# Batch 0's k and q loaded by longer pieces, turned in eighteen turns each, k ahead of p, and short products of zeros ahead of and between the turns

## The chip, the core and the metric

The kernel runs on one core of a Trainium2 chip. The metric is device time in microseconds (us), the median of several executions. The engines are named as in the profile: PE is TensorE's matmul, PEld its weight load, DVE is VectorE, ACT ScalarE, POOL GpSimd, SP the queue from which all DMAs are issued.

## The reference

Eight batches, eight heads, 576 tokens of 64 numbers. For each head a packed attention and an attention over its result, then a gated network over all tokens (x is 4608 x 512):

```
p_packed = sm_attn(p, k, v)              # p has 32 rows a head
out = sm_attn(q, p_packed, p_packed)
a = x @ w_a ;  b = x @ w_b               # 512 x 1536 each
return (a * b @ w_out)                   # 1536 x 512
```

All tensors are float32. The kernel keeps the exactness with products of high and low parts.

## The kernel before

Batches are worked on one after the other, the attention of the next batch beside the network of this one. The first stage of a batch (`stage1`) multiplies p by k, takes a softmax over 576 tokens and multiplies by v; the second (`stage2`) multiplies q by the packed result, takes a softmax over 32 and leaves its parts a_hi and a_lo. The network uses that the packed result has only 32 rows a head: `g_tiles` multiplies it by the weights (ghi, glo, two feature tiles at a time), and `mm1` multiplies ghi, glo by a_hi, a_lo. `mm2_part` is the product with w_out.

The weights come as 36 raw pieces of 512 KB, and each is turned into numbers by three steps, named by letters in the tables: A (`high_word`, on ACT), B (`low_word`, on ACT, DVE or POOL by the digit 0, 1 or 2 of `WAYS`) and C (`both_words`, on DVE). A `g_tiles` of two feature tiles needs the C of four pieces. The raw pieces have twelve buffers.

The order of every engine's queue is written out by hand. `FIRST` is the order of the loads on SP, `START` that of the work before the network begins, `PLAN_0` and `PLAN` that of the work between the half tiles of `mm1`. In `START`, k0 to k4 and q0 to q4 are the turns of k and q (`turn_first`: a PE turn of 128 columns against the identity `ident`, and copies on DVE or ACT by the digit of `TURN`), T0 and P0 the turns of p and of the packed result, S0 and S1 the first products of `stage1` for even and odd heads, r0 and r1 its later steps, s0 and s1 the steps of `stage2`, g the first `g_tiles`, and W nine products of 128x512 columns whose result nobody reads.

In PSUM x and m are pairs of buffers and s a single one of two banks. Batch 0 and 1 have their tokens in an order that `store_first` undoes when the results are written.

Of the kernel before, what the change touches and what calls it, by code (L numbers as in the profile page):

```python
# [8 lines left out]
F32 = mybir.dt.float32  # L9
# [10 lines left out]
def tile_packed_attn_gated_ffn(  # L20
# [72 lines left out]
    def bank():  # L93
        return ps_x.tile([P, 512], F32, name="x")
# [31 lines left out]

    firsts = {}

    def load_first(src, key, part):

        if part < 2:
            t = scratch.tile([P, R, 4 * D], F32, name=f"{key}n{part}")
            nc.sync.dma_start(
                out=t, in_=src[0, R * part:R * part + R, 0:4 * P, :].rearrange("h (p i) d -> p h (i d)", i=4))
        else:
            t = scratch.tile([P, H, 2 * D], F32, name=f"{key}n{part}")
            nc.sync.dma_start(out=t[0:TR], in_=src[0, :, 4 * P:S, :].rearrange("h (p u) d -> p h (u d)", u=2))
        firsts[key, part] = t  # L140

    def turn_first(key, n):

        if (0, key) not in xTs:
            pool = scratch if key == "q" else ld
            xTs[0, key] = [pool.tile([P, R, HS], F32, name=f"xT{i}") for i in range(2)]
        copy = (nc.vector.tensor_copy, nc.scalar.copy)[int(TURN["kq".index(key) * 5 + n])]
        x = bank_pair()[:, 0, :] if n in (2, 3) else bank()
        if n < 4:
            h = 2 * (n % 2)  # L150
            for i in range(4):
                nc.tensor.transpose(  # L152
                    x[:, P * i:P * i + P], firsts[key, n // 2][:, h + i // 2, P * (i % 2):P * (i % 2) + P], ident)
            copy(out=xTs[0, key][n // 2][:, h:h + 2, 0:2 * P], in_=x.rearrange("p (h t) -> p h t", h=2))
            return
        for h in range(H):
            nc.tensor.transpose(x[:, TR * h:TR * h + TR], firsts[key, 2][0:TR, h, :], ident[0:TR, 0:TR])
        for i in range(2):
            copy(out=xTs[0, key][i][:, :, 2 * P:HS], in_=x[:, P * i:P * i + P].rearrange("p (h t) -> p h t", h=R))
# [105 lines left out]
    def stage1(b, e):  # L265
# [185 lines left out]
    def store_first(ob, x, i):  # L451

        for u in range(2):
            if x < 8:
                rows = out[0:4 * P].rearrange("(a l i) n -> a i l n", a=4, i=4)[x % 4, 2 * (x // 4) + u]
            else:
                rows = out[4 * P:S].rearrange("(l u) n -> u l n", u=2)[u]
            nc.sync.dma_start(out=rows, in_=ob[i + TL * u:i + TL * u + TL])
# [68 lines left out]
    PLAN_0 = ("A | C C | B A B A | B C C B C | A A | C | B | C B A T0 k0 Lp2 A | A A B B C Lq0 | C C k1 | A B A | "  # L527
# [447 lines left out]
```

## Time and profile before

| | |
|---|---|
| median of 3 executions | 711.39 us (710.65 to 711.81) |
| the profiled execution: its own time, its span | 711.86 us, 710.1 us |
| PE busy | 696.6 us, 98% of the span |
| DVE, ACT, POOL busy | 451.5, 361.6, 418.2 us |
| first product of `mm1` | 35.14 us from the span's start |

The span runs from the first to the last instruction, and the time is some 1.8 us longer. A busy PE is one that has an instruction under way, which is not yet a PE at its peak. In the timelines a bracket at a row's end says how long the engine stood idle before the row, and what ended the wait. The chain that ended last lies on PE for 92% of the span and on DVE for 5%.

### The profile page before, as it was taken

The numbers are of one execution on the slowest core, as the hardware profiler recorded it, in microseconds if no ns is written. First come the engines' busy times: TensorE is split into PE (matmuls) and PEld (weight loads), VectorE is DVE, ScalarE is ACT, GpSimd is POOL, SyncE is SP. The second block draws the span as 40 slices with busy tenths as digits, with TensorE's granted clock in tenths as the row PEclk, the third lists the DMA queues.
The fourth block names the chain that finished last, engine by engine and source line by source line (L and its number), as shares of the span: only waits on it lengthen the run. The fifth ranks groups of instructions, "written<-read, shape, count | busy, mean of one in ns | idle before, by whom it ended". The sixth has DMA issues, their size and how long they took to land.

```text
span 710.1 us, 14172 instructions
## 1 busy us (share of the span) xinstructions
PE 696.6 (98%) x5546; PEld 573.4 (81%) x5546; DVE 451.5 (64%) x823; ACT 361.6 (51%) x729; POOL 418.2 (59%) x322
## 2 busy tenths in 40 slices
PE   5899999999999999999999999999999999999998
PEld 4488877888878878888888788788888888888886
DVE  3788755367456679665875678765785667754342
ACT  2788754454344455645554456555555446544420
POOL 0496753337334787745874589566775578856520
PEclk9999999999999999999999999999999999999999
DMA  8999967852344735546443563456245323133002
GB/s 250 386 270 308 259 114 247 247 112 90 93 114 141 207 86 158 135 125 152 141 102 123 148 184 93 122 171 159 75 110 169 105 90 119 60 111 127 1 1 74
DMA packets 181507, 102.63 MB, mean 145 GB/s; under 512 B 145728, under 2 KB 163904, under 8 KB 176064
## 3 DMA queue, kind: packets, MB, share of 16 engines
q1 hardware_dynamic: 181440, 101.73, 50.8%
q8 instruction: 43, 0.70, 0.4%
q14 instruction: 24, 0.20, 0.1%
HBM read 85.98 MB, written 15.73 MB: 143 GB/s over the span
## 4 chain that ended last, share of the span: by engine, by line
PE 92%; DVE 5%; issue 1%; ACT 1%; DMA 1%; SPq 0%; DVEq 0%; ACTq 0%
PE x L742 36%; PE m L784 27%; PE m L407 11%; PE m L433 5%; PE x L798 4%; PE s L319 2%; PE s L334 1%; PE x L389 1%; PE s L273 1%; DVE a_lo L91 1%; PE s L309 1%; DMA kn<-in_k_dram 1%; DVE part L752 1%; PE x L152 0%; PE m L152 0%
## 5 line engine op out<-in xcount | busy, mean ns | idle before, releaser
L742 PE MATMUL x<-wo,h_hi 128*128 128x512 f32 (+1 forms) x776 | 249.4, 391 | 0.0
L91 POOL TENSOR_TENSOR h_lo<-asb,h_hi 128x576 fp32r<-128x576 f32 x96 | 140.4, 1464 | 80.7 <-ACT h_hi L829 43.3
L742 PEld LDWEIGHTS x<-wo,h_hi 128*128 128x128 f32 x776 | 140.9, 188 | 22.0 <-ACT part L750 0.8
L742 PE MATMUL x<-wo,h_lo 128*128 128x512 f32 (+1 forms) x388 | 152.1, 392 | 0.0
L91 POOL TENSOR_TENSOR G_lo<-gs,G_hi 128x640 fp32r<-128x640 f32 x72 | 112.7, 1572 | 30.1 <-ACT G_hi L819 29.8
L742 PEld LDWEIGHTS x<-wo,h_lo 128*128 128x128 f32 x388 | 72.9, 188 | 11.7
L91 POOL TENSOR_TENSOR A_lo<-gs,A_hi 128x256 fp32r<-128x256 f32 x36 | 27.6, 766 | 89.6 <-ACT A_hi L807 89.6
L866 DVE TENSOR_TENSOR d<-m,d 128x576 f32<-128x576 f32 (+1 forms) x73 | 54.1, 741 | 34.7 <-ACT d L862 33.9
L879 DVE TENSOR_TENSOR asb<-m,d 128x288 f32<-128x288 f32 x72 | 32.5, 451 | 64.1 <-ACT c L875 60.7
L875 ACT COPY c<-m 128x288 f32<-128x288 f32 x72 | 28.8, 400 | 83.5 <-PE m L784 83.5
L752 DVE TENSOR_TENSOR part<-x,part 128x512 f32<-128x512 f32 (+1 forms) x65 | 44.1, 678 | 38.4 <-PE x L742 38.4
L784 PE MATMUL m<-tx_hi,G_hi 128*128 128x288 f32 x216 | 63.8, 295 | 0.0
L784 PE MATMUL m<-tx_hi,G_lo 128*128 128x288 f32 x216 | 63.6, 295 | 0.0
L784 PE MATMUL m<-tx_lo,G_hi 128*128 128x288 f32 x216 | 63.2, 293 | 0.0
L804 ACT COPY gs<-x 128x512 f32<-128x512 f32 x35 | 20.6, 588 | 81.9 <-PE x L798 80.6
L819 ACT CAST G_hi<-gs 128x640 fp32r<-128x640 f32 x72 | 52.2, 729 | 15.1 <-POOL gs L813 14.5
L862 ACT COPY d<-m 128x576 f32<-128x576 f32 (+1 forms) x73 | 46.7, 639 | 19.4 <-PE m L784 18.9
L829 ACT CAST h_hi<-asb 128x576 fp32r<-128x576 f32 x72 | 49.0, 680 | 11.5 <-DVE asb L893 11.5
L784 PEld LDWEIGHTS m<-a_hi,G_hi 128*128 128x128 f32 x144 | 27.0, 187 | 31.9 <-issue 17.4
L813 POOL TENSOR_TENSOR gs<-gs 128x512 f32<-128x512 f32 x36 | 46.6, 1293 | 2.9 <-DVE gs L810 2.8
L784 PE MATMUL m<-a_hi,G_hi 128*128 128x288 f32 x144 | 46.6, 324 | 0.0
L407 PE MATMUL m<-a_hi,ghi 128*128 128x288 f32 x192 | 43.2, 306 | 1.5 <-ACT ghi L395 1.5
(176 smaller groups left out, 1545.4 us busy)
## 6 DMA issues: line engine op xcount, KB each, us to landing
wr<-w_kept SPq DMA_DIRECT2D x36, 1024.0 KB, 5.0
nat<-in_k_dram SPq DMA_DIRECT2D x56, 144.0 KB, 4.7
nat<-in_q_dram SPq DMA_DIRECT2D x56, 144.0 KB, 5.3
vt<-in_v_dram SPq DMA_DIRECT2D x28, 256.0 KB, 3.9
out_dram<-part SPq DMA_DIRECT2D x27, 256.0 KB, 2.0
raw<-in_moe_w_a_dram SPq DMA_DIRECT2D x12, 512.0 KB, 7.7
raw<-in_moe_w_b_dram SPq DMA_DIRECT2D x12, 512.0 KB, 7.0
raw<-in_moe_w_out_dram SPq DMA_DIRECT2D x12, 512.0 KB, 7.2
```

The costliest lines, as they stand in the source:

```text
L91: return eng.tensor_tensor(out=dst, in0=src, in1=hi.bitcast(F32), op=ALU.subtract)
L407: nc.tensor.matmul(out=ps[:, half, 0:HS], lhsT=gt[:, kt, ft % 4, cols], rhs=at[:, kt, HS * half:HS * half + HS], start=(n == 0 and kt == 0 ...
L433: nc.tensor.matmul(out=o[:, cols], lhsT=ht[:, c0:c0 + P], rhs=wt[:, cols], start=(ft == 0 and n == 0), stop=(ft == NFT - 1 and n == 2))
L742: nc.tensor.matmul(out=o[:, cols], lhsT=ht[:, c0:c0 + P], rhs=wt[:, cols], start=(ft == fts[0] and n == 0), stop=end)
L752: nc.vector.tensor_tensor(out=parts[i][:, cols], in0=o[:, cols], in1=parts[i][:, cols], op=ALU.add)
L784: nc.tensor.matmul(out=bank[:, n % 2, 0:HS], lhsT=g, rhs=t, start=(first and i == 0), stop=(i == 2), skip_group_check=True)
L813: nc.gpsimd.tensor_tensor(out=gs[:, 2:4].rearrange("p a u f -> p a (u f)"), in0=gs[:, 0:2].rearrange("p a u f -> p a (u f)"), in1=s2.unsqu ...
L819: nc.scalar.copy(out=G_hi[:, n % 3], in_=gs[:, 1:6, n % 2])
L829: nc.scalar.copy(out=view(h_hi[ft]), in_=src)
L862: nc.scalar.copy(out=d[:, both], in_=X[:, both, 0:HS])
L866: nc.vector.tensor_tensor(out=d[:, both], in0=V[:, both, 0:HS], in1=d[:, both], op=ALU.add)
L879: nc.vector.tensor_tensor(out=hf[:, 1], in0=X[:, k0, 0:HS], in1=d[:, k0], op=ALU.mult)
```

## The change

The loads of k and q of batch 0 are two DMAs each in place of three: a partition holds a head and 36 neighbouring tokens, 16 of them (4 KB) by the first DMA and 20 (5 KB) by the second. All eighteen turns are now full 128x128 turns; before there were sixteen and eight of 32 rows. The copies write four or one neighbouring columns at a time in the order that the products want. k is loaded ahead of p. In `stage1` the last 32 columns of batch 0 are read with a step. W is gone; `wake` multiplies a tile of zeros by itself, 128x128, so many times as the number behind X, Y or Z says (into an x, s or m buffer): 24 times ahead of the first turn, nine in the first softmax, and 45 in the second stage. The tables START, PLAN_0, WAYS and TURN are new; B is on DVE for 15 pieces (7 before), on POOL for 5 (10) and on ACT for 16 (19). The stores of the first batch's results go in other pieces.

```diff
+    zero = scratch.tile([P, P], F32, name="zero")
+    nc.vector.memset(zero, 0.0)
...
     def load_first(src, key, part):
-        if part < 2:
-            t = scratch.tile([P, R, 4 * D], F32, name=f"{key}n{part}")
...
+        lo, n = ((0, 16), (16, 20))[part]
+        t = scratch.tile([P, n * D], F32, name=f"{key}n{part}")
+        rows = src[0].rearrange("h (g i) d -> (h g) (i d)", i=36)
+        nc.sync.dma_start(out=t, in_=rows[:, lo * D:(lo + n) * D])
...
     def turn_first(key, n):
+        pairs = [range(n, 8, 2), range(n, 8, 2), range(10, 18, 2), range(11, 18, 2), range(8, 10)][n]
+        for i, pair in enumerate(pairs):
+            c = P * (pair % 8 if pair < 8 else pair - 8)
+            nc.tensor.transpose(x[:, P * i:P * i + P], firsts[key, int(pair > 7)][:, c:c + P], ident)
         if n < 4:
+            m = pairs[0] // 2
+            out = wide[key][:, :, n % 2, :, m:m + 4]
+            copy(out=out, in_=x.rearrange("p (m h g) -> p h g m", m=4, h=H))
...
-    def warm(n=9):
+    def wake(kind, n):
-        x = bank_pair()[:, 0, :]
-        t = firsts["k", 0].rearrange("p h t -> p (h t)")
+        x = (bank() if kind == "X" else bank_pair(kind == "Y")[:, 0])[:, 0:P]
         for _ in range(n):
-            nc.tensor.matmul(out=x, lhsT=ident, rhs=t[:, 0:512], start=True, stop=True)
+            nc.tensor.matmul(out=x, lhsT=zero, rhs=zero, start=True, stop=True)
...
-    FIRST = ("p0 k0 k2 k1 q0 v0 q1 v1 q2 w1 w1 w1 w1 w1 w1 w1 w1 w1 w1 w1")
-    START = ("T0 k0 k4 k1 k3 k2 q0 S0 S1 r0 r1 q1 r1 r0 r0 r1 r0 q2 r1 q3 q4 P0 s0 B s1 W A s0 B A A s0 s0 B s1 C "
+    FIRST = ("k0 k1 p0 q0 q1 v0 v1 w1 w1 w1 w1 w1 w1 w1 w1 w1 w1 w1")
+    START = ("Y4 X6 X14 k0 k1 k2 T0 k3 k4 q1 S0 S1 r0 X4 r1 Z3 q0 r1 r0 Y2 r0 r1 q2 r0 r1 q3 q4 P0 s0 B s0 B X3 "
```

The queue of PE from the program's first instruction to the first softmax. Here p_nat, kn and qn are the loaded tiles, a row of the form `x<-ident,kn` is a turn, and `s<-xT,pT` or `s<-kT,pT` are S0's products. Before:

```order
L250 MATMUL x<-ident,p_nat 128x128 x2
L152 MATMUL x<-ident,kn_108 128x128 x4
L157 MATMUL x<-ident,kn_110 128x32 x8
L152 MATMUL x<-ident,kn_108 128x128 x4
L152 MATMUL m<-ident,kn_112 128x128 x8
L152 MATMUL x<-ident,qn_114 128x128 x4
L273 MATMUL s<-xT_154,pT 32x288 x2
```

And in the change:

```order
L591 MATMUL s<-zero 128x128 x4
L591 MATMUL x<-zero 128x128 x20
L152 MATMUL x<-ident,kn_107 128x128 x8
L152 MATMUL m<-ident,kn_109 128x128 x4
L250 MATMUL x<-ident,p_nat 128x128 x2
L152 MATMUL m<-ident,kn_109 128x128 x4
L152 MATMUL x<-ident,kn_109 128x128 x2
L152 MATMUL x<-ident,qn_114 128x128 x4
L280 MATMUL s<-kT,pT 32x256 x4
```

Twenty-four products of zeros stand at the head of the queue, p's turn has moved behind twelve of k's, and k takes 18 turns in place of 24.

The queue of PE from S1's last product to the turn of the first softmax (`a_0`). Before:

```order
L273 MATMUL m<-xT_155,pT 32x32 x2
L152 MATMUL x<-ident,qn_114 128x128 x4
L309 MATMUL x<-ident,a_0_228 128x128 x4
L310 MATMUL x<-ident,a_0_228 64x128
L309 MATMUL m<-ident,a_1_234 128x128 x4
L310 MATMUL m<-ident,a_1_234 64x128
L319 MATMUL x<-vt,a1T_247 32x64 x20
L152 MATMUL m<-ident,qn_120 128x128 x4
```

And in the change:

```order
L280 MATMUL m<-kT,pT 32x32 x4
L591 MATMUL x<-zero 128x128 x4
L591 MATMUL m<-zero 128x128 x3
L152 MATMUL x<-ident,qn_114 128x128 x4
L591 MATMUL s<-zero 128x128 x2
L316 MATMUL x<-ident,a_0_252 128x128 x4
L317 MATMUL x<-ident,a_0_252 64x128
L316 MATMUL m<-ident,a_1_263 128x128 x4
L317 MATMUL m<-ident,a_1_263 64x128
L152 MATMUL m<-ident,qn_116 128x128 x4
L326 MATMUL x<-vt,a1T_283 32x64 x20
L326 MATMUL x<-vt_122,a1T_293 32x64 x20
```

Nine products of zeros stand between S1 and the turn of `a_0`, around q0's turns, and q2's turns now stand ahead of both products with v.

The queue of PE from the second stage's first product to the first `g_tiles`, where `s<-xT,ppT` and `m<-xT,ppT` are `stage2` for even and odd heads. Before:

```order
L334 MATMUL s<-xT_191,ppT 32x288 x4
L334 MATMUL s<-xT_192,ppT 32x288 x4
L334 MATMUL m<-xT_191,ppT 32x288 x4
L334 MATMUL m<-xT_192,ppT 32x288 x4
L580 MATMUL m<-kn_108,ident 128x512 x9
L389 MATMUL x<-w_ab,ppT 32x512 x8
```

And in the change:

```order
L341 MATMUL s<-qT,ppT 32x288 x8
L591 MATMUL x<-zero 128x128 x3
L591 MATMUL m<-zero 128x128 x4
L591 MATMUL x<-zero 128x128 x2
L341 MATMUL m<-qT,ppT 32x288 x8
L591 MATMUL m<-zero 128x128 x30
L591 MATMUL x<-zero 128x128 x3
L591 MATMUL m<-zero 128x128 x3
L396 MATMUL x<-w_ab,ppT 32x512 x8
```

Nine products of zeros now stand between the even and the odd heads, and 36 of 128 columns stand where nine of 512 columns stood.

## Rows read from the trace of the kernel before

**Rows 1.** The page: busy time, share of the span and instructions of each engine, and the granted TensorE clock in 40 slices of the span, in tenths.

```profile
PE 696.6 (98%) x5546; PEld 573.4 (81%) x5546; DVE 451.5 (64%) x823; ACT 361.6 (51%) x729; POOL 418.2 (59%) x322
PEclk9999999999999999999999999999999999999999
```

**Rows 2.** The waits of PE from 36 us to the end: who waited for whom, us in total, times, the longest.

```profile
PE m L407 <- DVE a_lo L91: 0.3, 1, 0.3
PE m L784 <- DVE a_lo L91: 0.3, 1, 0.3
```

**Rows 3.** The timeline of PE from the start to `mm1`: start in us, length in us, engine, line, operation, out<-in, shape, count of the trace's instructions (a product of float32 that is no turn counts two), and the idle time before it.

```profile
7.14 1.11 PE L152 MATMUL x<-ident,kn 128*128 128x128 f32 x4 [2.48 <-DMA kn<-in_k_dram]
...
10.08 1.92 PE L152 MATMUL m<-ident,kn 128*128 128x128 f32 x8
11.79 1.06 PE L152 MATMUL x<-ident,qn 128*128 128x128 f32 x4
12.78 1.20 PE L273 MATMUL s<-xT,pT 64*32 64x288 f32 x22
...
14.84 0.66 PE L152 MATMUL x<-ident,qn 128*128 128x128 f32 x4
16.09 0.66 PE L309 MATMUL x<-ident,a 128*128 128x128 f32 x4 [0.60 <-ACT a L291]
...
16.94 0.66 PE L309 MATMUL m<-ident,a 128*128 128x128 f32 x4
17.43 0.27 PE L310 MATMUL m<-ident,a 128*64 128x128 f32 x1
17.64 0.90 PE L319 MATMUL x<-vt,a1T 128*32 128x64 f32 x40
18.47 0.66 PE L152 MATMUL m<-ident,qn 128*128 128x128 f32 x4
19.05 0.90 PE L319 MATMUL x<-vt,a1T 128*32 128x64 f32 x40
...
21.08 0.44 PE L259 MATMUL x<-ident,pp 128*128 128x128 f32 x2
22.13 0.72 PE L334 MATMUL s<-xT,ppT 64*32 64x288 f32 x16 [0.61 <-DVE ppT L261]
22.61 1.33 PE L334 MATMUL m<-xT,ppT 64*32 64x288 f32 x16
23.87 7.99 PE L580 MATMUL m<-kn,ident 128*128 128x512 f32 x18
32.10 1.57 PE L389 MATMUL x<-w_ab,ppT 64*32 64x512 f32 x16 [0.23 <-DVE w_ab L212]
35.14 0.53 PE L407 MATMUL m<-a_hi,ghi 128*128 128x288 f32 x2 [1.48 <-ACT ghi L395]
...
37.73 0.54 PE L407 MATMUL m<-a_lo,ghi 128*128 128x288 f32 x2 [0.27 <-DVE a_lo L91]
...
39.27 1.18 PE L389 MATMUL x<-w_ab,ppT 64*32 64x512 f32 x16
```

**Rows 4.** The timeline of DVE in the same stretch.

```profile
14.16 0.76 DVE L279 TENSOR_REDUCE nmx<-s 128x1 f32<-128x576 f32 x1 [1.44 <-PE s L273]
...
22.94 0.78 DVE L339 STREAM_TRANSPOSE s<-s 128x576 f32<-128x576 f32 x1 [0.96 <-PE s L334]
...
25.91 0.68 DVE L212 SCALAR_TENSOR_TENSOR w_ab<-raw 128x512 uint32<-128x512 uint32 x1
...
32.47 1.43 DVE L359 STREAM_TRANSPOSE a2f<-s 128x576 f32<-128x576 f32 x2
...
36.93 0.75 DVE L91 TENSOR_TENSOR a_lo<-a2f,a_hi 128x576 fp32r<-128x576 f32 x1
37.60 3.13 DVE L212 SCALAR_TENSOR_TENSOR w_ab<-raw 128x512 uint32<-128x512 uint32 x4
```

**Rows 5.** The timelines of ACT and POOL in the same stretch.

```profile
12.88 0.59 ACT L154 COPY xT<-x 128x512 f32<-128x512 f32 x1 [1.12 <-PE x L152]
15.21 0.74 ACT L291 ACTIVATE a<-s,nmx 128x576 f32<-128x576 f32 x1 [1.74 <-DVE nmx L280]
...
33.27 1.33 ACT L365 CAST a_hi<-a2f 128x576 fp32r<-128x576 f32 x2 [1.16 <-DVE a2f L359]
34.51 1.07 ACT L395 CAST ghi<-x 128x512 fp32r<-128x512 f32 x2
0.73 0.20 POOL masks.py:197 MEMSET ident<- 128x128 f32 x1 [0.29 <-POOLq L959]
```

**Rows 6.** The instructions on the tiles of k and q: duration in ns, least, median and greatest, first and last start in us; and how long k's DMAs took from issue to landing.

```profile
L580 PE MATMUL m<-kn,ident x18: 592/592/697, 23.9 to 31.3; 128*128 128x512 f32 x18
L152 PE MATMUL m<-ident,kn x8: 421/421/421, 10.1 to 11.6; 128*128 128x128 f32 x8
L152 PE MATMUL m<-ident,qn x8: 272/273/329, 18.5 to 20.3; 128*128 128x128 f32 x8
DMA to landing us min/median/max: 5.0/5.1/5.8
```

**Rows 7.** The timeline of SP's queue: the issue of k's first DMA.

```profile
2.12 0.61 SPq L135 DMA_DIRECT2D kn<-in_k_dram  x1
```

**Rows 8.** The step B on DVE over the whole kernel: duration in ns, least, median and greatest, first and last start in us.

```profile
L206 DVE TENSOR_SCALAR raw<-raw x7: 385/429/1656, 44.6 to 96.1; 128x512 uint32<-128x512 uint32 x7
```

More of the change, by code (lines that the diff above doesn't have):

```diff
@@ L125, in turn @@
         xTs.setdefault((b, key), []).append(xT)
-    firsts = {}
+    firsts, wide = {}, {}
     def load_first(src, key, part):
-        if part < 2:
-            t = scratch.tile([P, R, 4 * D], F32, name=f"{key}n{part}")
[L135 to L139, printed above, removed]
+        lo, n = ((0, 16), (16, 20))[part]
+        t = scratch.tile([P, n * D], F32, name=f"{key}n{part}")
+        rows = src[0].rearrange("h (g i) d -> (h g) (i d)", i=36)
+        nc.sync.dma_start(out=t, in_=rows[:, lo * D:(lo + n) * D])
         firsts[key, part] = t
@@ L144, in turn_first @@
         if (0, key) not in xTs:
-            pool = scratch if key == "q" else ld
-            xTs[0, key] = [pool.tile([P, R, HS], F32, name=f"xT{i}") for i in range(2)]
+            t = scratch.tile([P, H, HS], F32, name=f"{key}T")
+            xTs[0, key] = [t[:, 0:R], t[:, R:H]]
+            wide[key] = t.rearrange("p h (z g m) -> p h z g m", z=2, m=9)
         copy = (nc.vector.tensor_copy, nc.scalar.copy)[int(TURN["kq".index(key) * 5 + n])]
         x = bank_pair()[:, 0, :] if n in (2, 3) else bank()
+        pairs = [range(n, 8, 2), range(n, 8, 2), range(10, 18, 2), range(11, 18, 2), range(8, 10)][n]
+        for i, pair in enumerate(pairs):
+            c = P * (pair % 8 if pair < 8 else pair - 8)
+            nc.tensor.transpose(x[:, P * i:P * i + P], firsts[key, int(pair > 7)][:, c:c + P], ident)
         if n < 4:
[L150 to L159, printed above, removed]
+            m = pairs[0] // 2
+            out = wide[key][:, :, n % 2, :, m:m + 4]
+            copy(out=out, in_=x.rearrange("p (m h g) -> p h g m", m=4, h=H))
+        else:
+            copy(out=wide[key][:, :, :, :, 4].rearrange("p h z g -> p z h g"),
+                 in_=x[:, 0:2 * P].rearrange("p (z h g) -> p z h g", z=2, h=H))
     vts, p_nat = {}, {}
@@ L270, in stage1 @@
         parts = [(0, 0, 0, HS)] + ([(1, TR, 0, 2 * P), (1, 0, 2 * P, TR)] if first else [(1, 0, 0, HS)])
+        if b == 0:
+            parts = [(u, (TR * u, 2 * P - 2 * P * u)[i], i, (2 * P, TR)[i]) for u in range(2) for i in range(2)]
         for u, c, t, n in parts:
             for r in range(R):
+                if b == 0:
+                    cols = xT_cols(0, "k", u, 2 * r + e).rearrange("d (z p) -> d z p", z=2)
+                    cols = cols[:, :, P:].rearrange("d z k -> d k z") if t else cols[:, :, 0:P]
+                else:
+                    cols = xT_cols(b, "k", u, 2 * r + e, slice(t, t + n))
                 nc.tensor.matmul(
                     out=s[J * r:J * r + J, u, c:c + n], lhsT=pT[64 * u:64 * u + 64, 2 * r + e, :],
-                    rhs=xT_cols(b, "k", u, 2 * r + e, slice(t, t + n)), start=True, stop=True)
+                    rhs=cols, start=True, stop=True)
         s = s[:, :, 0:HS]
@@ L439, in store @@
         if b == 0:
-            for i in range(2):
-                store_first(ob, c0 // 64 + i, 64 * i)
+            for i in range(4):
+                x, u = divmod(c0 // TL + i, 2)
+                store_first(ob, HS * u + TL * x, TL * i, TL)
             return
@@ L445, in store @@
         if b == 1 and c0 == 0:
-            store_first(ob, 0, 0)
+            for u in range(2):
+                store_first(ob, HS * u, TL * u, TL)
             parts = parts[1:]
@@ L449, in store, with store_first @@
             nc.sync.dma_start(out=out[t:t + n, cols], in_=ob[i:i + n, cols])
[L451 to L458, printed above, removed]
+    def store_first(ob, c, i, n):
+        half = HS // 2
+        while n:
+            uz, p0 = divmod(c, half)
+            m = min(n, half - p0)
+            rows = out[0:S].rearrange("(p z u) n -> u z p n", z=2, u=2)[uz // 2, uz % 2, p0:p0 + m]
+            nc.sync.dma_start(out=rows, in_=ob[i:i + m])
+            c, i, n = c + m, i + m, n - m
     def out_tile(i):
@@ L481, in emit @@
                 continue
-            if name == "W":
-                warm()
+            if name[0] in "XYZ":
+                wake(name[0], int(name[1:]))
                 continue
@@ L515, in tile_packed_attn_gated_ffn @@
     st = {}
-    FIRST = ("p0 k0 k2 k1 q0 v0 q1 v1 q2 w1 w1 w1 w1 w1 w1 w1 w1 w1 w1 w1")
-    START = ("T0 k0 k4 k1 k3 k2 q0 S0 S1 r0 r1 q1 r1 r0 r0 r1 r0 q2 r1 q3 q4 P0 s0 B s1 W A s0 B A A s0 s0 B s1 C "
-             "A s1 B s0 C s1 A s1 C B B Lp2 C A B A s0 s1 B C B B s0 B g A C A A s1 Lv2 Lk2 C C A A C B B Lk3 C s1")
-    WAYS = ("000000022220202120012012011200010010")
-    TURN = ("0001110101")
+    FIRST = ("k0 k1 p0 q0 q1 v0 v1 w1 w1 w1 w1 w1 w1 w1 w1 w1 w1 w1")
+    START = ("Y4 X6 X14 k0 k1 k2 T0 k3 k4 q1 S0 S1 r0 X4 r1 Z3 q0 r1 r0 Y2 r0 r1 q2 r0 r1 q3 q4 P0 s0 B s0 B X3 "
+             "A Z4 A s0 X2 s1 Z30 B A X3 B C s0 B s1 s1 s0 C s1 Lk2 A B A C A Z1 C Z2 A A s0 s1 s1 C C B s0 g B "
+             "s1 B Lp2 C B A s1 B Lk3 A C")
+    WAYS = ("100002021121200111211010011001010010")
+    TURN = ("1110101111")
     SUBS = ("0100")
```

2 lines of the change are left out of this document (1 added, 1 removed), and 7 rows, old and new, of the table PLAN_0.

## The prediction

> **What bounds the kernel.** I read the page first: PE is busy 98% of the span [rows 1]. Then the waits of PE from 36 us on: there are two, of 0.3 us [rows 2]. So from `mm1` on PE's queue is full and sets the end, and a change to the work before `mm1` is worth what it moves `mm1`, unless it opens new holes behind. Then the timelines of the first 40 us. k lands at 7.14 us; its turns fill PE until the first product of `stage1` at 12.78; the first softmax and the products with v fill it until 21.5; the second softmax is a DVE chain from 22.94, and the first weights' product waits for C until 32.10 [rows 3, 4]. `mm1` starts at 35.14 when ghi is there, waits once for a_lo (37.73), and comes to the second weights' product at 39.27 [rows 3]. That point, from which PE never starves again, is my mark.
>
> **TensorE's clock.** The granted clock reads 1.00 throughout [rows 1], but the durations tell two levels. A turn lasts 421 ns at 10 to 12 us and 273 at 18 to 20 [rows 6]; in a run they follow at (11.79 - 10.08) / 8 = 0.214 us early and (17.43 - 16.94) / 4 = 0.122 later [rows 3]. That is the lower (1.2 GHz) and the higher level (2.4). Turns alone from 7.14 to 12.78 did not bring the higher one; it was there by 14.84, where four turns take 0.66 us in place of 1.06 [rows 3], after S0 and S1, the first products that are no turns. The Trainium skill says so too (TensorE: Matmul & The Clock Gate, section Part 4: PE-mode transpose): transposes do not count as a busy PE as products do. By that rule too the zeros would bring the higher level earlier.
>
> **The change, part by part.**
>
> *A product of zeros.* W is eighteen rows in 7.99 us [rows 3]: 0.444 for 512 columns, 0.111 for 128, two rows a product: 0.222 us. That is the lower bound, at the lower level 0.444 (turns in a run at 0.214 a row make 0.43). The upper bound is two of the turns in short groups, with their switching: (19.05 - 18.47) / 4 = 0.145, so 0.29, and (12.78 - 11.79) / 4 = 0.25, so 0.50 at the lower level [rows 3]. I take 0.23 and 0.43: runs of 20 and 30 equal products are nearest to W and to the run of eight turns.
>
> *The 24 ahead of k.* They can start when the tile of zeros is written, which I put at 1.0 us as POOL's fill of an equal tile is done at 0.93 [rows 5]. When does the level rise? Bounds: 2.1 us after the first product, if S0's start at 12.78 to 14.84 was all it took, or 7.7 us, if everything since 7.14 counted. I take 3 us, near the first, since zeros are products and no turns; so 4.0: 3.0 / 0.43 = 7 slow products, then 17 x 0.23 = 3.9; PE is free at 7.9 us.
>
> *k ahead of p, in longer pieces.* k's DMA was issued at 2.12 and landed 5.0 later [rows 6, 7]; moved to the queue's head at about 0.74 it lands at 5.7, the second some 2 us later, by 7.7. Both are hidden by the 24 products. q and v are earlier too, and nobody waits for them here. The copies write strided; the trace shows no copy of this kind, and I give it the 0.59 of ACT's copy [rows 5]. At double that three copies on ACT would add 1.8 us at most ahead of S0, part of it behind turns.
>
> *Turns to S0.* Eighteen of k and two of p, the last copy behind them: 20 x 0.14 + 0.27 to the last turn's end + 0.4 for its copy = 3.45, so S0 starts at 11.35; before, 12.78: **-1.43**.
>
> *S0 to the first softmax's turn.* Before 16.09 - 12.78 = 3.31. After, PE's own queue decides: S0 and S1 at the higher level 0.55 each (S2's sixteen rows took 22.61 - 22.13 = 0.48, and four short ones are added), nine products 2.07, four turns of q 0.56: 3.73. The data would be there at 0.95 + 1.93 = 2.88 (0.95 is S2's 22.94 - 22.13 and something for the short ones; 1.93 is 16.09 less DVE's maximum at 14.16). **+0.42**.
>
> *From there to the second softmax.* Before 22.94 - 16.09 = 6.85. q2's turns fill the time in which ACT copies, and q4 is two turns in place of eight: P0 comes after the softmax's own turns (twice five, 1.48), q2 (0.58), the two products with v (2 x (18.47 - 17.64) = 1.66), q3 (0.58) and q4 (0.3): 4.6, in place of 21.08 - 16.09 = 5.0. What follows is the same. I put it at **-0.45**.
>
> *Nine zeros between even and odd heads.* The odd product starts 0.5 + 9 x 0.23 = 2.57 after the even, DVE can read it 0.81 later (22.94 - 22.13), so 2.57 us after DVE's first transpose starts. DVE, which now takes one C (0.6) before it, is free after (25.91 - 22.94) / 2 + 0.6 = 2.1 [rows 4]. It stands for **+0.46**, and all the rest of its queue, which holds the same instructions up to a_lo, comes that much later. B on DVE costs 0.43 [rows 8]; the first lies in DVE's wait for the second stage, and two of the next stand before the C that the second weights' product waits for: **+0.1** of their 0.86, since that product needs the last C only for its second half.
>
> *The 36 zeros in W's place.* They begin 0.5 + 2.57 - 0.81 = 2.26 us after that transpose and last 36 x 0.23 = 8.3; with 1.2 for the weights' product ghi can be cast at 11.7. ACT gets to it only behind both a_hi and now a B: the odd heads' a2f ends 32.47 + 1.43 - 22.94 = 11.0 after the transpose, a_hi and B take 0.66 each, so 12.3, + 0.46 = 12.8 [rows 4, 5]. So they are hidden, by 1.1 us.
>
> The sum: -1.43 + 0.42 - 0.45 + 0.46 + 0.1 = **-0.9 us**. Against the profiled execution (711.86, 0.47 above the median) that is 711.0, against the median 710.5. The stores go out beside PE work and are put at nothing.
>
> **Rivals.**
>
> *No product so cheap (slower, 0.20).* At 0.29 and 0.50: PE free at 4.0 + 18 x 0.29 = 9.2, S0 at 12.65 (-0.1), the softmax's turn 1.1 + 2.6 + 0.56 = 4.3 later (+1.0), then -0.45; the 36 zeros end 0.5 + 0.5 - 0.81 + 45 x 0.29 = 13.2 after the transpose, the weights' product at 14.4, `mm1` 0.6 later, the mark 3.3 later at 18.3, in place of 39.27 - 22.94 = 16.3: +2.0. In all +2.4: 713.8. It decides from about 0.25 on; from 0.26 the 36 zeros are no longer hidden, and each 0.01 costs 0.45 there. For it: every short group of turns in the trace. Against: the longer runs. The Trainium skill's rule (same page, section Back-to-back issue gap) is that products of 128 columns with their weight loads follow at 81 ns rather than 56; an estimate by that ratio is 0.222 x 1.45 = 0.32 us a product, and the time would be some 715.
>
> *Clock early, products at 0.222 (faster, 0.34).* The level rises 2.1 us in: 4.7 slow products, 19.3 x 0.222 = 4.3; PE free at 7.4. That is -0.5 more, and 18 products on the path save 0.15: 709.8. For it: S0 to 14.84 is 2.1 at most. Against: turns may have counted for something.
>
> *Same within the measurement, 0.2% or 1.4 us either way (0.46).* The forecast, **710.5**; its own range is 710.0 to 712.8. The new tables could also open a hole behind the mark, since DVE takes eight B more (3.4 us); that would be in this case or the slower one.
>
> **The numbers.** 710.5; 8 in 10 between 709.0 and 713.4: the early clock with some more, and the dear product. Faster 0.34, same 0.46, slower 0.20.
>
> **What would show it.** S0 near 11.3 us with turns at 273 ns from the first one; the 24 zeros' end near 7.9; the first softmax's turn following the zeros at once, without a wait for ACT; DVE idle about half a microsecond before its second transpose; the first weights' product done before ACT has cast a_hi; the second weights' product at about 38.4. The prediction is wrong if the zeros end after 9 us, if the level has not risen when k's turns begin, or if PE shows waits for DVE or ACT between 40 and 100 us.

## The result, and the profile after

The changed kernel takes 716.38 us (median of four executions, 715.17 to 718.24) against 711.36 for the kernel before in the same session: a ratio of 1.0074 [1.005, 1.0098]. It is slower by 5 us, with an interval clear of 1, and outside the range of 709.0 to 713.4. The profiled execution took 716.74 us with a span of 715.0, 4.9 more than the span before.

From the page of the changed kernel, the line of PE and the granted clock in 40 slices, which answer to [rows 1]:

```profile
PE 705.8 (99%) x5688; PEld 588.5 (82%) x5688; DVE 457.0 (64%) x829; ACT 361.9 (51%) x727; POOL 407.2 (57%) x317
PEclk9989999999999999999999999999999999999999
```

PE is busy a larger share than before and yet ends later, and one slice, the third (about 36 to 54 us), no longer reads 9. The waits of PE in the changed kernel from 33 us on, against [rows 2]:

```profile
PE m L414 <- ACT ghi L402: 2.9, 1, 2.9
PE m L414 <- DVE asb L429: 0.5, 1, 0.5
PE m L795 <- DVE a_lo L93: 0.3, 1, 0.3
```

The wait for ghi ahead of `mm1` was 1.48 us before [rows 3] and is 2.9 now, and a wait for asb behind the mark is new (asb is the tile into which ACT and DVE take `mm1`'s result out of PSUM). PE's timeline in the changed kernel, columns as in [rows 3]:

```profile
1.05 2.07 PE L591 MATMUL s<-zero 128*128 128x128 f32 x8 [1.05 <-DVE zero L77]
2.92 5.67 PE L591 MATMUL x<-zero 128*128 128x128 f32 x40
8.42 1.04 PE L152 MATMUL x<-ident,kn 128*128 128x128 f32 x8
...
11.58 0.71 PE L280 MATMUL s<-kT,pT 64*32 64x256 f32 x25 [0.19 <-ACT kT L158]
...
15.55 0.60 PE L316 MATMUL x<-ident,a 128*128 128x128 f32 x4
...
24.35 6.96 PE L591 MATMUL m<-zero 128*128 128x128 f32 x60
...
32.58 1.09 PE L396 MATMUL x<-w_ab,ppT 64*32 64x512 f32 x16
36.53 0.85 PE L414 MATMUL m<-a_hi,ghi 128*128 128x288 f32 x2 [2.86 <-ACT ghi L402]
37.17 0.68 PE L414 MATMUL m<-a_lo,ghi 128*128 128x288 f32 x2
...
42.59 1.09 PE L396 MATMUL x<-w_ab,ppT 64*32 64x512 f32 x16
```

Two things are to be seen. Up to the second softmax all is near the forecast, and its first product (20.85) is 1.3 us ahead of the kernel before (22.13). Then `mm1` starts at 36.53 in place of 35.14, and its first 24 products take 42.59 - 36.53 = 6.06 us, where they took 39.27 - 35.14 = 4.13, a wait included [rows 3]. The windows of the changed kernel say why (window in us; its length, then busy us of PE, PEld, DVE, ACT, POOL with counts, granted clock, DMA share, GB/s):

```profile
30.00:35.00 5.00, 3.67 (x40) 2.64 (x39) 4.86 (x9) 1.37 (x3) 4.84 (x3) 1.00 0.94 222
35.00:40.00 5.00, 3.47 (x14) 3.47 (x15) 5.00 (x10) 3.12 (x6) 3.46 (x2) 0.58 0.97 287
40.00:45.00 5.00, 5.00 (x38) 3.88 (x37) 3.29 (x6) 3.23 (x6) 0.69 (x1) 0.74 1.12 339
45.00:50.00 5.00, 5.00 (x40) 5.00 (x38) 4.67 (x7) 4.49 (x9) 2.28 (x2) 1.00 0.87 159
```

With the hole of 2.86 us the granted clock falls: 0.58 is the mean of a stretch that is partly at full speed. Products then follow at 0.48 us a pair, the lower level (1.2 GHz), until it is back at 1.00. The hole's source is DVE's queue. The timelines of DVE, ACT and POOL in the changed kernel:

```profile
21.67 0.79 DVE L346 STREAM_TRANSPOSE s<-s 128x576 f32<-128x576 f32 x1 [0.85 <-PE s L341]
...
24.52 0.78 DVE L346 STREAM_TRANSPOSE s<-m 128x576 f32<-128x576 f32 x1 [0.68 <-PE m L341]
...
27.98 3.25 DVE L212 SCALAR_TENSOR_TENSOR w_ab<-raw 128x512 uint32<-128x512 uint32 x3
...
33.94 0.78 DVE L366 STREAM_TRANSPOSE a2f<-s 128x576 f32<-128x576 f32 x1
34.75 0.67 ACT L372 CAST a_hi<-a2f 128x576 fp32r<-128x576 f32 x1 [2.13 <-DVE a2f L366]
35.33 0.68 ACT L209 ACTIVATE raw<-raw 128x512 uint32<-128x512 uint32 x1
35.91 1.05 ACT L402 CAST ghi<-x 128x512 fp32r<-128x512 f32 x2
28.21 1.41 POOL L362 TENSOR_TENSOR s<-s,sum 128x576 f32<-128x576 f32 x1 [3.35 <-ACT raw L201]
```

Three C take 3.25 us, where one takes 0.68 [rows 4]: they meet POOL's product of two inputs (28.21 to 29.62). Their durations (ns, least, median and greatest; first and last start in us):

```profile
L212 DVE SCALAR_TENSOR_TENSOR w_ab<-raw x3: 627/1134/1649, 28.0 to 30.1; 128x512 uint32<-128x512 uint32 x3
```

The second, from 28.5 on, lasts 1.65 us; the third, 1.13, runs beside the B that POOL does next. The second a2f, and with it a_hi, a B (35.33, L209) and ghi on ACT, come later.

Where the 4.9 us went: the mark (the second weights' product) stands at 42.59 in place of 39.27, +3.3, and from the mark to the span's end it is 672.4 in place of 670.8, +1.6.

### The profile page after: what moved, and what is told of

It reads as the page before. It is cut to its first block, busy times and chain, and to the rows that moved or that the text cites. A ratio compares the mean times of both kernels' runs of the same rounds, so it can differ in the third digit from the quotient of the medians.

```text
span 715.0 us, 14450 instructions
## 1 busy us (share of the span) xinstructions
PE 705.8 (99%) x5688; PEld 588.5 (82%) x5688; DVE 457.0 (64%) x829; ACT 361.9 (51%) x727; POOL 407.2 (57%) x317
## 4 chain that ended last, share of the span: by engine, by line
PE 92%; DVE 5%; issue 1%; DMA 1%; ACT 1%; DVEq 0%; SPq 0%
PE x L753 36%; PE m L795 27%; PE m L414 10%; PE m L440 5%; PE x L809 4%; PE s L326 2%; PE s L341 1%; PE x L396 1%; PE x L591 1%; PE s L280 1%; DVE a_lo L93 1%; PE s L316 1%; DMA nat<-in_q_dram 1%; DVE w_ab L212 1%; DVE xT L126 0%
```

## The experiments

All runs in one table. The ratio is against the kernel before in the same session, whose median was 711.82 for e1 to e5, 711.19 for e6 to e9 and 711.93 for e10 to e13; medians of different sessions differ by such amounts too. Span, mark and the rest behind the mark are of the profiled execution, in us, which for e2 (718.8) and e11 (715.28) is among the slowest of its run.

| run | median | ratio [95%] | span | mark | mark to end |
|---|---|---|---|---|---|
| before (profile shown) | 711.36 | 1 | 710.1 | 39.27 | 670.8 |
| the change | 716.38 | 1.0074 [1.005, 1.0098] | 715.0 | 42.59 | 672.4 |
| e1_fill_hole | 715.28 | 1.005 [1.0038, 1.0063] | 713.8 | 40.12 | 673.7 |
| e2_b_tail | 717.91 | 1.0091 [1.0076, 1.0107] | 717.0 | 41.49 | 675.5 |
| e3_before_tail | 711.37 | 0.9993 [0.9984, 1.0001] | 710.0 | 38.90 | 671.1 |
| e5_c_later | 715.03 | 1.0045 [1.0031, 1.0059] | 713.5 | 40.33 | 673.2 |
| e6_before_plan | 715.35 | 1.0057 [1.0044, 1.0069] | 713.5 | 42.23 | 671.3 |
| e7_no_mid_zeros | 710.69 | 0.9991 [0.9982, 1.0] | 708.5 | 37.47 | 671.0 |
| e8_no_first | 708.84 | 0.9967 [0.9954, 0.9979] | 707.4 | 36.25 | 671.2 |
| e9_no_w | 712.12 | 1.0018 [1.0008, 1.0027] | 711.0 | 40.23 | 670.8 |
| e10_no_zeros_head | 708.66 | 0.9957 [0.9945, 0.9969] | 706.7 | 35.21 | 671.5 |
| e11_after_no_first | 713.79 | 1.0025 [1.0016, 1.0034] | 713.5 | 40.98 | 672.5 |
| e12_plan_and_fill | 714.66 | 1.004 [1.0027, 1.0053] | 712.9 | 40.93 | 672.0 |
| e13_c_beside | 709.78 | 0.9967 [0.9956, 0.9978] | 708.0 | 37.31 | 670.7 |

The first four ask where the loss sits. The theory was that the clock's fall in the hole is the main part; the rivals were the order behind the mark and the B that went to DVE.

### e1_fill_hole

```diff
-  ... s0 s1 s1 C C B s0 g B s1 B Lp2 ...
+  ... s0 s1 s1 C C B s0 g Z12 B s1 B Lp2 ...
```

> The changed kernel with twelve more products of zeros behind the first weights' product, ahead of mm1: twelve at the 0.227 us of the thirty are 2.7 us, and the hole in which PE stands idle there is 2.86 us. Theory 1, the clock: that hole lets the clock fall, and mm1's first 24 products run at the lower level (0.48 us a pair in place of 0.27, 6.06 us in place of some 3.4). Filled, the granted clock stays at 1.00, the second weights' product starts near 40.1 us in place of 42.6, and the median falls from 716.4 to some 714. Theory 2, the queues of DVE and ACT: mm1's late start (36.5) is the whole loss and PE would wait for a_lo or C in the same places anyhow; then the clock is back but a_lo (38.4) and C (39.4 and 40.4) hold mm1, and the median stays within 1 us of 716.4.

Twelve products of zeros now stand in the hole. The window from 35 to 40 us of this run:

```profile
35.00:40.00 5.00, 5.00 (x38) 4.53 (x36) 5.00 (x10) 3.60 (x8) 3.40 (x2) 1.00 1.03 272
```

And its timeline of PE:

```profile
33.52 2.94 PE L591 MATMUL m<-zero 128*128 128x128 f32 x24
36.45 0.53 PE L414 MATMUL m<-a_hi,ghi 128*128 128x288 f32 x2
...
40.12 1.34 PE L396 MATMUL x<-w_ab,ppT 64*32 64x512 f32 x16
```

The clock stays at 1.00 with `mm1` at the same place, the first 24 products take 3.67 us, and the mark comes 2.5 earlier. That much is the clock's in these two traces. But the rest behind the mark grows by 1.3: PE now waits there twice, where the change waits once, by the list of its waits in this run:

```profile
PE m L414 <- ACT asb L426: 0.8, 1, 0.8
PE m L414 <- DVE asb L429: 0.5, 1, 0.5
```

The new wait of 0.8 is most of the 1.3: a faster PE comes earlier to results that DVE and ACT deliver no earlier. In the median 1.1 us are left, with intervals that overlap; the spans agree (713.8 against 715.0). Of the change's own four executions one has a mean granted clock of 1.000 and a span of 713.4, the others 0.995 and 714.2 to 715.0; the five of e1 have 1.000 and 713.2 to 713.8.

### e2_b_tail

```diff
-    WAYS = ("100002021121200111211010011001010010")
+    WAYS = ("100002021120202120012012011200010010")
```

> The changed kernel with the digits of B of the kernel before from the twelfth piece on (eight B go back from DVE to POOL or ACT), all else as changed; the work ahead of mm1 is the same. Theory: B on DVE overfills DVE's queue between 50 and 70 us (9.4 and 10.0 of 10 us busy) and makes PE wait 0.5 us for asb and 1 us for C; then these waits go, the stretch from the second weights' product to the end falls from 672.4 to 670.9 us as before, and the median falls by 1.5 us to some 714.9. Rival: the two transposes of the next batch's k, which stand earlier on DVE now, fill it and not B; then the waits stay and the median is within 0.5 us of 716.4.

The digits of the kernel before from the twelfth piece on do not make it better: 717.91, with an interval that overlaps the change's. The waits of PE in this run:

```profile
PE m L414 <- DVE asb L429: 1.8, 2, 1.3
PE m L414 <- ACT asb L426: 0.6, 1, 0.6
```

PE waits longer for asb with the B back on ACT and POOL. The new orders were written for the new digits, so this alone does not clear B on DVE; e6 below does. Which instruction is late here was not followed.

### e3_before_tail

```diff
-  ... q3 q4 P0 s0 B s0 B X3 A Z4 A s0 X2 s1 Z30 ... g B s1 B Lp2 C B A s1 B Lk3 A C
+  ... q3 q4 P0 s0 B s1 Z36 A s0 B A A s0 s0 B s1 C A s1 B s0 C ... g A C A A s1 Lv2 ...
   (with WAYS and PLAN_0 of the kernel before)
```

> The changed loads, turns, zeros and order up to the turn of the packed result, and behind it the order, the digits of B and the plan of the kernel before, with 36 products of zeros in the place of its nine products of 512 columns. Theory: the changed head is worth what it moved the second softmax, 22.94 to 21.67, or 1.3 us, and the loss lies wholly in the order behind; then the second weights' product starts near 38.0 us, PE waits nowhere behind it, and the median is 710.1. Rival: the new loads, the strided copies and products or the stores of the first batch cost something of their own that the head hides; then the median is 711.4 or more.

The new loads, turns and zeros up to P0 with the old tables behind: 711.37 against 711.82, no difference that this measurement can tell. Its timeline of PE at `mm1` is that of the kernel before again:

```profile
34.77 0.53 PE L414 MATMUL m<-a_hi,ghi 128*128 128x288 f32 x2 [1.47 <-ACT ghi L402]
...
38.90 1.19 PE L396 MATMUL x<-w_ab,ppT 64*32 64x512 f32 x16
```

So the whole loss of the change lies in the tables behind P0, and its head gains nothing that shows. The new loads, stores and products are in this run too, and the stretch behind the mark is 671.1 against 670.8. This opens the second question: why the head, with k earlier and fewer turns, is worth nothing.

### e5_c_later

```diff
-  ... s0 B s1 s1 s0 C s1 Lk2 A B A C A Z1 C Z2 A A s0 s1 s1 C C B s0 g B
+  ... s0 B s1 s1 s0 s1 s1 Lk2 A B A A Z1 Z2 A A s0 s1 C C C C C B s0 g B
```

> The changed kernel with three of the C ahead of a_hi moved behind both a2f, away from POOL's product of the first softmax (28.2 to 29.6 us); the sum and product of the odd heads stand in their place. Theory: two C took 1.3 us each there in place of 0.63 because POOL's two-input product ran beside them; away from it all five take 0.63 to 0.68, both a2f come some 2.5 us sooner, the first weights' product follows the C at about 33.5 us, mm1 starts near 35.3, the hole ahead of it is under 1.5 us and the clock does not fall; the second weights' product starts near 39.3 and the median falls by 3 us to some 713.4. Rival: the C were slow for another reason (ACT's A beside them, the loads), they stay slow wherever they stand, mm1 starts at 36.5 or later, and the median is 716 or more.

The three C stand behind both a2f. Timelines of DVE and PE in this run:

```profile
32.49 3.65 DVE L212 SCALAR_TENSOR_TENSOR w_ab<-raw 128x512 uint32<-128x512 uint32 x5
36.27 0.53 PE L414 MATMUL m<-a_hi,ghi 128*128 128x288 f32 x2 [0.69 <-ACT ghi L402]
```

And the five C one by one, columns as above:

```profile
L212 DVE SCALAR_TENSOR_TENSOR w_ab<-raw x5: 677/679/1151, 32.5 to 35.5; 128x512 uint32<-128x512 uint32 x5
```

Away from POOL's product, beside POOL's B, most C take 0.68 again and one 1.15. (The expectation put two C of the change at 1.3 each; they are 1.65 and 1.13.) The hole shrinks to 0.69, the clock stays at 1.00 and the mark comes at 40.33. But the first weights' product now waits 0.8 for its C, so `mm1` starts 36.27 - 22.16 = 14.1 us after DVE's first transpose in place of 14.9 (12.2 in e3), and the rest behind the mark grows by 0.8.

### e6_before_plan

```diff
-  ... g B s1 B Lp2 C B A s1 B Lk3 A C
+  ... g B s1 B Lp2 Lv2 C B A s1 B Lk3 A C A A B B C C
   (with PLAN_0 of the kernel before)
```

> The changed kernel with the plan of the kernel before for the work between the half tiles of mm1 (PLAN_0); two A, B and C and one load of v are put at START's end, as many as that plan takes for done. The digits of B and the work ahead of mm1 are as changed. Theory: the loss behind the second weights' product (1.6 us in the changed kernel, 2.9 with the hole filled) is the changed plan's, which has 17 C done at its tenth step where the plan before has 20, and two transposes of k side by side; then PE waits nowhere between 45 and 100 us, that stretch takes 671 us again, and the median is 716.4 - 1.6 = 714.8 or less. Rival: the eight B that are on DVE now overfill it under any plan; then the waits for asb and C between 55 and 70 us stay, and the median is 716 or more.

The waits of PE in this run from 33 us on:

```profile
PE m L414 <- ACT ghi L402: 2.9, 1, 2.9
PE m L794 <- DVE a_lo L93: 0.3, 1, 0.3
```

Behind `mm1`'s start PE waits nowhere but for the 0.3 us at the end that all runs have; the rest behind the mark is 671.3, 1.1 less than in the change, with the clock's fall still there (0.74 in 35 to 40 us). The digits of B are the new ones here, so B on DVE does not make PE wait by itself. So the new PLAN_0, with the end of START that goes with it, costs about 1 us behind the mark.

### e12_plan_and_fill

```diff
-  (e6) ... C C B s0 g B s1 ...
+       ... C C B s0 g Z12 B s1 ...
```

> The changed kernel with the plan of before (715.35) and the hole ahead of mm1 filled with twelve products of zeros. Theory: the clock's fall and the plan's waits are two losses that add; with both gone mm1's first 24 products take some 3.5 us in place of 4.9 to 6.1, PE waits nowhere behind, and the median is 713.0 to 713.8. What is left above 711.4 is the order of START alone: mm1's start at 36.5 in place of 35.1. Rival: with the clock back PE comes to asb and C before they are there, as when the hole alone was filled, and gains less than 0.7: 714.7 or more.

Both remedies together: clock 1.00, no waits behind the mark, and still 714.66. The medians fell by 0.7 from e6, by the ratios 1.0057 and 1.004 by 1.2. Against the kernel before in its own session the change loses 5.0 us, e1 3.5, e6 4.2 and this run 2.7: gains of 1.6, 0.9 and 2.3, so the two remedies add up as far as the intervals tell, and both are worth less than was expected of them. What is left against e3 (2.9 us of span) lies mostly at `mm1`'s start: 37.28 in this trace against 34.77, with nearly the same S0 (12.31 and 12.49). That is the order in START itself, which no filler mends.

### e8_no_first

```diff
-  (e3) Y4 X6 X14 k0 k1 k2 T0 ...
+       k0 k1 k2 T0 ...
```

> The same base (the changed head, order and plan of before behind it, median 711.4) without the 24 products of zeros ahead of k's turns. Theory: the zeros buy the higher level for k's turns and S0 and pay for it by holding them from k's landing (some 5.5 us) to 8.4 to 9.3; without them the turns run at the lower level (421 ns, 0.22 to 0.25 us apart) from about 5.6, S0 starts near 11 us in place of 11.6 to 12.5 but at the lower level, and the median is within 0.7 us of 711.4. Rival 1: the zeros are a pure delay; S0 starts near 9.5, and the median falls by 2 us or more. Rival 2: without them the level stays low into the first softmax; the median rises by 1 us or more.

Without the 24 products of zeros ahead of k the kernel beats both: 708.84, 0.9967. PE's timeline of this run:

```profile
4.61 1.94 PE L152 MATMUL x<-ident,kn 128*128 128x128 f32 x8 [4.61 <-DMA kn<-in_k_dram]
...
8.90 1.01 PE L152 MATMUL x<-ident,qn 128*128 128x128 f32 x4
9.84 0.71 PE L280 MATMUL s<-kT,pT 64*32 64x256 f32 x26
```

k is there at 4.6 us, and in the change its turns start at 8.42, because the zeros hold PE. The turns run at the lower level, but S0 is at the higher one from its first product. The zeros buy a clock that the turns bring by themselves, and cost the wait. Against the kernel before in its own session this run gains 2.35 us, and e3, with the 24, 0.45: the 24 cost about 1.9.

### e11_after_no_first

```diff
-  (the change) Y4 X6 X14 k0 k1 k2 T0 ...
+               k0 k1 k2 T0 ...
```

> The changed kernel as it is, without the 24 products of zeros ahead of k's turns. Theory: they are a pure delay here too; S0 starts near 9.8 us in place of 11.6, all up to mm1 moves with it, and the median falls by 2 to 2.5 us, from 716.4 to some 714. Rival: the weights' pieces arrive and are converted no sooner, so that C holds mm1 or the plan's holes behind it grow; then the median is 715.5 or more.

The same in the change itself: 713.79, 2.6 less in the medians, 3.2 against each session's kernel before. S0 starts at 9.90 (11.58), and the hole ahead of `mm1` stays (2.8 us, granted clock 0.50 in 35 to 40 us). So the delay at the head is there with either order behind it.

The twelve executions of this one kernel also price the clock's fall: five with a mean granted clock of 1.000 have spans of 710.1 to 711.6 us, six at 0.997 to 0.998 have 712.0 to 712.5, and the profiled one, at 0.995, has 713.5. The clock falls in some executions and not in others, and where it falls it is worth 1 to 2 us at the end.

### e7_no_mid_zeros and e10_no_zeros_head

```diff
-  (e3) S0 S1 r0 X4 r1 Z3 q0 r1 r0 Y2 r0 r1 q2 ...
+       S0 S1 r0 r1 q0 r1 r0 r0 r1 q2 ...
   (e10: also without Y4 X6 X14)
```

> The changed head with the order and plan of before behind it (median 711.4) without the nine products of zeros in the first softmax (X4, Z3, Y2). Theory: PE's own queue holds the first softmax's turn there, 3.97 us after S0 where the data are there after 2.9; without the nine it comes 1.0 us sooner and so does all behind it up to mm1: median 710.4. Rival: without them the clock falls in the softmax's gaps, and the products with v and the second stage run at the lower level; then the gain is lost and the median is 711.4 or more.

> The changed loads and turns with the order and plan of before behind them, and no product of zeros at all ahead of the second stage (neither the 24 nor the nine in the first softmax); the 36 in W's place stay. Theory: the 24 were a pure delay and the nine a small one (0.27 us up to the second stage, 0.7 in the medians); the median is 708.2 to 708.6, the best so far. Rival: the nine are what holds the level once the 24 are gone; then S1, the products with v or the second stage show the lower level (the second stage's sixteen rows over 0.5 us) and the median is 709.5 or more.

Without the nine zeros between S1 and the first softmax's turn that turn comes 14.17 - 11.33 = 2.84 us after S0 (3.97 in the change), but the second stage only 0.27 earlier after S0 than in e3: the rest is lost again in between, where was not followed. 710.69 against e3's 711.37 cannot be told apart. Without any zeros ahead of the second stage 708.66, the best of all, though not distinguishable from e8; both beat the kernel before, and the change by more than 7 us. PE's timeline of e10:

```profile
8.35 0.63 PE L152 MATMUL x<-ident,kn 128*128 128x128 f32 x2
8.77 0.64 PE L152 MATMUL x<-ident,qn 128*128 128x128 f32 x4
9.68 0.71 PE L280 MATMUL s<-kT,pT 64*32 64x256 f32 x25 [0.27 <-ACT kT L158]
```

Nothing but turns has run by 8.77, and the four turns of q take 0.64 us, the higher level (in e8 the same four still take 1.01). So turns alone brought it.

### e9_no_w

```diff
-  (before) ... s0 B s1 W A s0 B ...
+           ... s0 B s1 A s0 B ...
```

> The kernel before without its W, the nine products of 512 columns between the second stage and the first weights' product; nothing reads their result, so the output is the same. PE then stands idle from 23.9 to 32.1 us. Theory: an idle PE loses the higher level, as in the changed kernel's 2.86 us hole; the granted clock falls below 1.00 ahead of mm1, its first 24 products take some 6 us in place of 4.1, the second weights' product starts near 41.2 and the median rises by about 2 us to 713.5. Rival: the clock fell in the changed kernel for another reason (the zeros themselves); then mm1 runs at 0.27 us a pair here too and the median stays at 711.4.

What the fillers between the second stage and the weights' product are worth: 712.12, +0.9 against its own session. PE stands idle 8.06 us, and the windows of this run show the price:

```profile
25.00:30.00 5.00, 0.00 (x0) 0.00 (x0) 4.83 (x11) 4.98 (x9) 2.10 (x2) 0.62 1.05 387
30.00:35.00 5.00, 3.01 (x18) 0.99 (x19) 4.94 (x8) 3.81 (x8) 4.84 (x3) 0.50 1.06 388
35.00:40.00 5.00, 5.00 (x23) 5.00 (x22) 5.00 (x8) 4.14 (x8) 4.84 (x3) 0.51 1.07 366
```

`mm1`'s first 24 products take 40.23 - 34.43 = 5.8 us at the lower level, where the kernel before takes 4.13. The second stage happened to start 0.77 earlier in this trace (21.36 against 22.13), so the mark moved by 1.0 only. In the change a hole a third as long goes with as slow a start of `mm1` (6.06). Ahead of S0 this kernel has run turns alone, and S0's first products are at the higher level, 0.72 us in place of 1.20 [rows 3]:

```profile
12.49 0.72 PE L273 MATMUL s<-xT,pT 64*32 64x288 f32 x23
```

### e13_c_beside

```diff
-  (e8) ... C A s1 B s0 C s1 A s1 C B B Lp2 ...
+       ... C A s1 B s0 C C s1 A s1 B B Lp2 ...
```

> The faster kernel (changed loads and turns, no 24 zeros, order and plan of before: 708.84) with one C moved forward on DVE, so that it stands behind another C and runs while POOL's product of the first softmax runs (25.6 to 27.0 us); nothing else moves. Theory: DVE's two-input C is held while POOL's two-input product runs; this C takes 1.1 to 1.65 us in place of 0.63, both a2f come 0.5 to 1.0 us later, and the median is 709.4 to 709.9. Rival: the slow C of the changed kernel had another cause; it takes 0.65 here too and the median stays at 708.8.

One C is moved beside POOL's product, in the kernel that is otherwise the fastest but one. The two C in that place in this run (ns, least, median and greatest; first and last start in us):

```profile
L212 DVE SCALAR_TENSOR_TENSOR w_ab<-raw x2: 627/1136/1644, 25.0 to 25.6; 128x512 uint32<-128x512 uint32 x2
```

POOL's product in its timeline:

```profile
25.28 1.41 POOL L362 TENSOR_TENSOR s<-s,sum 128x576 f32<-128x576 f32 x1 [2.83 <-DVE sum L361]
```

And the windows around `mm1`, columns as above:

```profile
30.00:35.00 5.00, 3.53 (x19) 2.62 (x15) 5.00 (x9) 4.47 (x8) 4.84 (x3) 0.74 1.07 367
35.00:40.00 5.00, 5.00 (x43) 3.99 (x43) 5.00 (x7) 3.55 (x7) 4.26 (x3) 0.92 1.11 342
```

The second C starts at 25.6, while POOL's product runs to 26.69, and lasts 1644 ns: it ends 0.55 after POOL, about its own length. That fits a C that waited for POOL to finish. The median is 0.9 above e8's and the mark 1.06 later, but not all of it is the C: `mm1` starts 0.57 later behind DVE's first transpose (32.40 - 19.64 against 32.13 - 19.94), and its first 24 products take 4.91 in place of 4.12, since the clock fell here too. The holes were 0.60 and 1.47 us with half a weights' product between; in e8 0.50 and 1.47, and no fall. By the ratios, 0.9967 both, a loss at the end is not shown; the longer C is.

## Why the prediction was wrong, point by point

**Right.** *A product of zeros*: 0.227 us at the higher level (24.35 to the end of thirty at 31.15) and 0.467 at the lower ((2.92 - 1.05) / 4), against 0.23 and 0.43. The rival "no product so cheap" had the right sign by a mechanism that did not occur; the Trainium skill's ratio (TensorE: Matmul & The Clock Gate, section Back-to-back issue gap), 0.32 by my estimate, did not occur either. *The 24 ahead of k*: PE free at 8.42 against 7.9. *S0*: 11.58 against 11.35; *S0 to the softmax's turn* 3.97 against 3.73; *nine zeros*: DVE idle 0.68 against 0.46. *DVE's first transpose* came at 21.67, 1.27 earlier than before against the forecast 1.46. That agreement is partly luck: two of its terms came out 0.2 too late, and the third, from the softmax's turn to that transpose, 0.3 sooner than forecast (6.12 against 6.40).

**Wrong: "k ... lands at 5.7, the second ... by 7.7. Both are hidden by the 24 products."** k landed at 4.5 to 4.6 (e8, e10) and both parts 3.6 to 4.9 us after their issue. The 24 products therefore did not hide a wait but were one: about 1.9 us by e8 and e3, 2.6 to 3.2 by e11 and the change. I had taken them for part of the gain.

**Wrong: "Turns alone from 7.14 to 12.78 did not bring the higher one."** The rows are right, the conclusion is not: e8 and e9 have S0 at the higher level after turns, and e10 has it during the turns. In the profile before, the rise merely came while S0 and S1 ran. The Trainium skill's rule that the prediction cites (TensorE: Matmul & The Clock Gate, section Part 4: PE-mode transpose), that transposes do not count as a busy PE as products do, is not borne out here; e10's 0.64 us for four turns at 8.77 decides against it. One profile with one transition could not carry a rule of cause.

**Wrong: "all the rest of its queue, which holds the same instructions up to a_lo, comes that much later."** The instructions are the same, but their neighbours are not: C moved beside POOL's product of two inputs and took 3.25 us for three, 1.2 more than three at 0.68 [rows 4]. The Trainium skill has the rule (SBUF — State Buffer, section Who interferes with whom): an instruction of DVE with two SBUF inputs and one of GpSimd that reads SBUF share a read port, and the later one waits for the other's end. The 1649 ns in the change and the 1644 in e13 agree with it. Beside POOL's B, which reads SBUF too, most of e5's C keep to 0.68 us and one takes 1.15, which that rule alone would not give.

**Wrong: a B on ACT that is in the working and not in the sum.** The part on the 36 zeros has a_hi and a B of 0.66 each ahead of ghi and puts ghi's cast 12.8 us after DVE's first transpose. The kernel before has it at 34.51 - 22.94 = 11.57 [rows 4, 5], so the working says +1.2 at `mm1`, and the sum takes +0.46 and +0.1. The B, put at nothing there without a reason, measured 0.58 (35.33 to 35.91).

**Wrong: "So they are hidden, by 1.1 us."** The 36 zeros were hidden, but I counted the hole behind them as free. It became 2.86 us (DVE's delay above, a_hi and a B on ACT ahead of ghi), and an idle PE lost the higher level: 6.06 in place of 4.13 us for `mm1`'s first products. e1 shows the size, 2.5 us at the mark, and e11's executions what of it reaches the end, 1 to 2 us. No rival contained it: I had looked at the clock only where it rises.

**Wrong: +0.1 for the B and nothing for the new tables behind the mark.** There 1.6 us were lost. The prediction named such a hole as possible, for the eight B on DVE; but with these B and the old PLAN_0 (e6) PE has no such wait, and 1.1 of the 1.6 come back. The stores, put at nothing, did cost nothing that shows (e3).

**The account, by the profiled executions.** Head: 2.4 gained by the new loads and turns, which were not taken apart (e8, 711.19 to 708.84), about 2 of it spent on the 24 zeros (e3 stands at -0.4). Tables behind P0, against e3: `mm1` 14.86 us after DVE's first transpose in place of 12.21 (+2.65), its first 24 products +1.93, behind the mark +1.3. The sum 2.65 + 1.93 + 1.3 = 5.9, less 0.9 by which that first transpose was earlier than in e3's trace (21.67 against 22.56), is 5.0: the difference of the spans 715.0 and 710.0. These are places in one trace and not what each would give back alone, as e1 and e5 show.

The 2.65 can be read from the rows, with the kernel before, where it is 12.20, beside it. The second a2f ends 34.72 - 21.67 = 13.05 us after the first transpose in place of 33.90 - 22.94 = 10.96 [rows 4]; of these 2.1 us DVE's wait for the odd heads behind the nine zeros is 0.68, and the longer C are 1.2. `mm1` follows that a2f by 1.81 in place of 1.24 [rows 3, 4], which is the B on ACT. Of these three only the C was moved by itself (e5), and there the first weights' product waited 0.8 for its C, so that no more than 0.75 came back. Open are what is late in e2 and what holds the second stage in e7.

## What to carry to other kernels

A hole on PE has two prices, its length and the clock behind it: when a sum puts work "hidden by a microsecond", ask whether PE is idle there and for how long, not only whether it waits. Carry every delay of the working into the sum. Filler that warms TensorE paid here only where PE would wait anyway, and then less than the clock it kept (e1); ahead of the first data, compare it with the landing time of that data, and with what the real work brings by itself. When an order changes, look up each moved DVE instruction with two inputs for what POOL runs beside it, since its duration is not its own. And try the parts of a change apart: the new loads and turns, with no zeros ahead of the second stage and the old tables behind, beat the kernel before by 3.3 us (e10).

## What was not expected of the hardware

- With 2.86 us without work on PE (the change) the granted clock fell, to a mean of 0.58 in 35 to 40 us. After 1.48 (before), after 0.50 and 1.47 (e8) and after 0.78 and 0.69 (e5) it did not; after 0.60 and 1.47 (e13) it did. It was back at 1.00 by 45 us in the change, with PE busy throughout from 36.53.
- The same hole does not always cost the same: behind 2.8 to 2.9 us `mm1`'s first 24 products took 4.70 us in e2, 4.91 in e6, 6.03 in e11 and 6.06 in the change, and five of e11's twelve executions show a mean clock of 1.000 (of these no trace was kept, so that their hole is the same is taken and not shown).
- The view of the granted clock reads 1.00 from the start in the change (0 to 5 us), where products of zeros still follow at 0.467 us. At the start of a span the level shows only in durations, which also holds for the prediction's "1.00 throughout" (its rows are in tenths, where 9 is 0.90 or more).
- The rise varies from trace to trace for the same instructions: the 24 zeros ended at 8.42 (the change), 9.32 (e3), 9.15 (e12) and 8.17 (e7). That is 1.1 us of spread in single profiles which no edit explains, and a reason to read gains at the head from the medians.
- k's two DMAs with pieces of 4 and 5 KB, at the head of SP's queue, landed 3.6 to 4.9 us after issue; before, three DMAs with shorter pieces behind p took 5.0 to 5.8 [rows 6]. The place in the queue goes with it rather than the pieces: q's two in the change have the same pieces, stand behind p, and took 4.8 to 5.8. From the change, k's and then q's:

```profile
DMA to landing us min/median/max: 3.6/4.3/4.9
DMA to landing us min/median/max: 4.8/5.3/5.8
```
